# Sliding-window attention followed by a spectral mixing layer, on one core: a fixed engine order, full-size value and spectrum matmuls, paired transposes and one mask table

## The chip, the core and the metric

One core of a Trainium2 chip runs the whole program. The metric is device time in microseconds (us), the median of several runs. A run is "fast" or "slow" (slow: over 1.5% above the fastest of the same kernel); all runs quoted here are fast ones. The names of the engines in the profile are PE (TensorE, matmuls), PEld (its weight loads), DVE (VectorE), ACT (ScalarE), POOL (GpSimd) and SP (the DMA queue). SBUF is the on-chip memory in which the program keeps its tiles, PSUM the one that takes the results of matmuls.

## The reference, cut to what matters

```python
# q, k, v: (8 batches, 8 heads, 576 positions, 64); 64 modes; d_model 512
scores = q @ k.T / 8 + alibi_bias          # only 0 <= i - j < 128 is kept
attn   = softmax(scores);  x = (attn @ v), heads joined: (8, 576, 512)
X = rfft(x, axis=1)[:, :64]
Y = einsum('bmd,mde->bme', X, w_r + 1j*w_i)     # 64 modes, 128 MB of float32 weights
u = x + irfft(Y, n=576)
out = u + relu(u @ w_ch)
```

## The kernel before

The program has three stages. **Attention** goes through 16 units, each of one batch and four heads (a batch is two units), and fills `x` and then the spectrum `XC`. The **modes** stream 128 weight tiles of 1 MB through eight buffers. The **finish** makes the output tiles. In attention the engines' instructions are ordered by a scheduler; only the DMA queue's order is fixed (`manual_schedule(engines={SP})`).

```python
# the loop of attention; unit u is scored while unit u-1 takes its values
for u in range(n + 1):
    if u + 2 < n: at.load(u + 2)
    if u < n and (u % 2 == 1 or u == n - 2): load_w()
    if u < n:     at.scores(u, (0, 1))         # PE scores, ACT exp, DVE mask multiply
    if u + 1 < n: at.casts(u + 1)              # POOL: q, k, v to bf16
    if u > 0:     at.values(u - 1, 0)          # PE values, DVE normalise
    if u + 1 < n: at.transposes(u + 1, 0)      # PE transposes of q, ACT copy
    if u < n:     at.scores(u, (2, 3))
    if u > 0:     at.values(u - 1, 1)
    if u + 1 < n: at.transposes(u + 1, 1)      # PE transposes of k, DVE copy
    if u > 0 and u % at.NG == 0: at.spectrum(u // at.NG - 1)

def casts(self, u, eng=None):                  # cut
    (eng or nc.gpsimd).tensor_copy(qc, qr); (eng or nc.gpsimd).tensor_copy(kc, kr)
    vb = self.vb[u % 3]                        # three v buffers, freed by values()
    nc.gpsimd.tensor_copy(vb[:, :FULL, :, :D], vr[:, :FULL])
    nc.gpsimd.tensor_copy(vb[:TAIL, FULL, :, :D], vr[:TAIL, FULL])

# scores, per key tile kt:
nc.scalar.activation(att[:, kt], sc, AF.Exp, scale=1.0 / math.sqrt(D))
nc.vector.tensor_tensor(out=att[:, kt], in0=att[:, kt], in1=mask..., op=ALU.mult)

# values: after the full-width tiles of a head, the last 64 queries
nc.tensor.matmul(av[row, h, 260:325], lhsT=att[:, FULL-1, e, h*256+P : h*256+192], ...)
nc.tensor.matmul(av[row, h, 260:325], lhsT=att[:TAIL, FULL-1, e, h*256+192 : h*256+256], ...)
```

The softmax here doesn't subtract the row's maximum and nothing guards it: scores larger than these inputs give would overflow.

## Time and profile before

The median is 579.49 us (578.26 to 580.91, 4 runs). The stage borders are read from the timeline and from the instructions of the weight tiles.

| Stage, from the profiles | before | after |
|---|---|---|
| attention, until the first mode's matmul starts | 213.9 us | 199.0 us |
| modes, until the last weight tile's last matmul starts | 307.8 us | 310.2 us |
| finish, until the end | 55.5 us | 52.7 us |

Part 2 of the page of the kernel before cuts the span into 40 slices of 14.4 us. PEclk is the granted clock of PE in tenths (9 is 90% or more), DMA the busy tenths of the DMA engines. Part 4 says which work made up the chain that ended last.

```profile
PEclk9996655555555559786687889798877867676999
DMA  9998657759520019999999999999999999990666
...
DMA 42%; PE 32%; DVE 14%; ACT 6%; POOL 2%; issue 2%; SPq 0%; POOLq 0%; ACTq 0%
DMA w<-in_moe_w_i_dram 41%; PE acc L418 6%; DVE att L229 4%; PE av L249 4%; ACT att L227 3%; PE sc L222 3%; PE xt L289 3%; PE tp L197 2%; PE av L254 2%; PE av L258 2%; DVE x_full L268 2%; PE av L245 2%; PE zz L447 1%; PE mm L474 1%; DVE Zs L455 1%
```

From the sixteenth slice on DMA is full: the modes wait for weights, 41% of the span. The two zeros just before are a hole in which nothing is loaded, because all eight weight buffers are full and attention has not ended. So the modes' stream can't start earlier than attention's end, and what attention saves, the program saves.

The next view gives busy us of each engine in stretches of the kernel before (columns in its second line): two of attention, one of the modes.

```profile
core 0: us, PE busy (x) PEld busy (x) DVE busy (x) ACT busy (x) POOL busy (x), PEclk, DMA share, GB/s
100.00:120.00 20.00, 15.80 (x183) 11.02 (x179) 12.47 (x22) 10.27 (x11) 7.22 (x7) 0.50 0.77 229
120.00:140.00 20.00, 15.81 (x157) 10.32 (x156) 12.30 (x26) 8.34 (x10) 6.87 (x7) 0.50 0.65 198
230.00:250.00 20.00, 12.25 (x50) 5.26 (x49) 2.46 (x6) 1.73 (x4) 0.00 (x0) 0.74 1.01 423
```

No engine is full in attention, and PE's granted clock is 0.50. It is a loop of waits: scores, exp, mask, values, normalise, copies. A batch takes about 24 us (20.9 to 25.1 from the start of one batch's spectrum to that of the next, but for the last).

PE's timeline within the values of one head (start, length, what): the full-width matmuls follow each other every 50 to 60 ns, and each of the two 64-wide ones (L254, L258), and the first full-width one after them, comes 180 to 190 ns after its forerunner.

```profile
101.17 0.24 PE L245 MATMUL av<-vb_131,att 128*128 128x65 bf16 x1
101.23 0.25 PE L249 MATMUL av<-vb_131,att 128*128 128x65 bf16 x1
101.41 0.26 PE L254 MATMUL av<-vb_131,att 128*64 128x65 bf16 x1
101.60 0.26 PE L258 MATMUL av<-vb_131,att 64*64 64x65 bf16 x1
101.79 0.24 PE L249 MATMUL av<-vb_131,att 128*128 128x65 bf16 x1
```

The Trainium skill (TensorEngine Tiling (Array Packing), Key Properties) says that changing the tiling mode drains TensorE. The trace fits this, and adds a size: at half clock about 130 ns more than the usual spacing for each change. That all of it is the drain was not separated.

DVE's timeline at the start of the kernel before: a copy of 128x768 took 0.54 us once, and 5.88 us the next time, when POOL ran casts one after the other beside it. The first scores had to wait for the copy behind it. The last line is a mask multiply of the steady part, with no cast on POOL beside it: 0.69 us.

```profile
13.53 0.54 DVE L154 COPY maskB<-maskA 128x768 bf16<-128x768 bf16 x1
14.36 5.88 DVE L154 COPY maskB<-maskA 128x768 bf16<-128x768 bf16 x1 [0.29 <-POOL maskA L147]
20.17 1.34 DVE L201 COPY qkT_134<-tp 128x1152 bf16<-128x1152 bf16 x1
...
114.31 0.69 DVE L229 TENSOR_TENSOR att<-att,maskA 128x1024 bf16<-128x1024 bf16 x1
```

### The profile page before, as it was taken

The numbers are of one execution on the slowest core, as the hardware profiler recorded it, in microseconds if no ns is written. First come the engines' busy times: TensorE is split into PE (matmuls) and PEld (weight loads), VectorE is DVE, ScalarE is ACT, GpSimd is POOL, SyncE is SP. The second block draws the span as 40 slices with busy tenths as digits, with TensorE's granted clock in tenths as the row PEclk, the third lists the DMA queues.
The fourth block names the chain that finished last, engine by engine and source line by source line (L and its number), as shares of the span: only waits on it lengthen the run. The fifth ranks groups of instructions, "written<-read, shape, count | busy, mean of one in ns | idle before, by whom it ended". The sixth has DMA issues, their size and how long they took to land.

```text
span 577.3 us, 6872 instructions
## 1 busy us (share of the span) xinstructions
PE 398.7 (69%) x2677; PEld 208.6 (36%) x2694; DVE 208.7 (36%) x385; ACT 153.3 (27%) x214; POOL 91.7 (16%) x115
## 2 busy tenths in 40 slices
PE   1387679787788768477567646767664766666884
PEld 1255456555555534233233322323322322222331
DVE  5766666755656562101110111232011000003665
ACT  4344433453335403011001101221110100002554
POOL 5622242433231020000000000000000000000444
PEclk9996655555555559786687889798877867676999
DMA  9998657759520019999999999999999999990666
GB/s 255 297 274 263 197 150 237 243 132 246 154 108 1 1 68 398 423 419 422 423 419 422 420 421 421 421 421 357 423 422 421 422 420 423 421 396 20 212 209 217
DMA packets 71089, 173.48 MB, mean 301 GB/s; under 512 B 41360, under 2 KB 41360, under 8 KB 54672
## 3 DMA queue, kind: packets, MB, share of 16 engines
q1 hardware_dynamic: 71056, 173.03, 79.7%
q8 instruction: 21, 0.34, 0.2%
q14 instruction: 12, 0.10, 0.1%
HBM read 163.58 MB, written 9.44 MB: 300 GB/s over the span
## 4 chain that ended last, share of the span: by engine, by line
DMA 42%; PE 32%; DVE 14%; ACT 6%; POOL 2%; issue 2%; SPq 0%; POOLq 0%; ACTq 0%
DMA w<-in_moe_w_i_dram 41%; PE acc L418 6%; DVE att L229 4%; PE av L249 4%; ACT att L227 3%; PE sc L222 3%; PE xt L289 3%; PE tp L197 2%; PE av L254 2%; PE av L258 2%; DVE x_full L268 2%; PE av L245 2%; PE zz L447 1%; PE mm L474 1%; DVE Zs L455 1%
## 5 line engine op out<-in xcount | busy, mean ns | idle before, releaser
L418 PE MATMUL acc<-w,XC 128*32 128x512 bf16 x512 | 140.4, 452 | 56.9 <-DMA w<-in_moe_w_i_dram 32.9
L418 PEld LDWEIGHTS <-XC 128*32 128x32 bf16 x512 | 55.6, 141 | 122.6 <-issue 102.4
L227 ACT ACTIVATE att<-sc 128x1024 bf16<-128x1024 f32 x64 | 61.9, 1028 | 54.7 <-PE sc L222 54.7
L498 POOL TENSOR_TENSOR r<-r,x_full 128x512 f32<-128x512 f32 x16 | 18.5, 1157 | 338.1 <-ACT r L494 332.7
L427 DVE CAST yq<-acc 128x512 bf16<-128x512 f32 x16 | 11.1, 692 | 166.6 <-PE acc L418 166.6
L474 PE MATMUL mm<-wch,xT 128*128 128x512 bf16 x133 | 44.0, 455 | 9.2 <-DVE xT L471 8.9
L249 PEld LDWEIGHTS <-att 128*128 128x128 bf16 x256 | 25.6, 122 | 45.0 <-DVE x_tail L274 27.1
L229 DVE TENSOR_TENSOR att<-att,maskA 128x1024 bf16<-128x1024 bf16 x48 | 37.3, 777 | 12.1 <-ACT att L227 11.7
L476 ACT CAST XW<-mm 128x512 bf16<-128x512 f32 x36 | 21.1, 586 | 76.7 <-PE mm L474 76.7
L471 DVE COPY xT<-tr 128x512 bf16<-128x512 bf16 x36 | 15.3, 425 | 71.1 <-PE tr L469 71.1
L436 ACT COPY YT<-tr 128x128 bf16<-128x128 bf16 x8 | 5.8, 728 | 99.4 <-DVE YT L436 99.4
L469 PE MATMUL tr<-ident,x_full 128*128 128x128 bf16 x128 | 16.7, 272 | 18.9 <-ACT YT L439 12.6
L503 DVE TENSOR_TENSOR o<-yy,r 128x512 f32<-128x512 f32 x36 | 23.5, 687 | 14.8 <-POOL r L498 12.2
L222 PE MATMUL sc<-qkT_134 64*128 64x256 bf16 (+2 forms) x160 | 17.4, 361 | 15.8 <-DVE qkT_134 L201 13.0
L439 ACT COPY YT<-tr 128x64 bf16<-128x64 bf16 x16 | 5.8, 530 | 81.3 <-DVE YT L439 77.8
L474 PEld LDWEIGHTS <-xT 128*128 128x128 bf16 x144 | 12.8, 109 | 34.5 <-DVE xT L471 21.8
L494 ACT ACTIVATE r<-mm 128x512 f32<-128x512 f32 x36 | 21.1, 597 | 14.8 <-PE mm L483 11.3
L469 PEld LDWEIGHTS <-x_full 128*128 128x128 bf16 x128 | 13.2, 124 | 29.2 <-issue 19.5
L289 PE MATMUL xt<-F,x_full 128*128 128x128 bf16 x128 | 19.6, 308 | 5.5 <-DVE qkT_135 L201 4.2
L197 PE MATMUL tp<-ident,qc 128*64 128x128 bf16 x288 | 19.0, 314 | 5.5 <-DVE qc L183 5.5
L249 PE MATMUL av<-vb_131,att 128*128 128x65 bf16 x96 | 14.6, 242 | 11.5 <-DVE x_tail L274 10.3
L268 DVE TENSOR_TENSOR x_full<-av,rec 128x512 bf16<-128x512 f32 x32 | 22.0, 689 | 0.6
(109 smaller groups left out, 557.2 us busy)
## 6 DMA issues: line engine op xcount, KB each, us to landing
w<-in_moe_w_r_dram SPq DMA_DIRECT2D x64, 1024.0 KB, 15.4
w<-in_moe_w_i_dram SPq DMA_DIRECT2D x64, 1024.0 KB, 16.6
qr<-in_q_dram SPq DMA_DIRECT2D x16, 576.0 KB, 4.9
kr<-in_k_dram SPq DMA_DIRECT2D x16, 576.0 KB, 5.6
vr<-in_v_dram SPq DMA_DIRECT2D x64, 128.0 KB, 3.4
out_dram<-o SPq DMA_DIRECT2D x32, 256.0 KB, 2.1
vr<-in_v_dram SPq DMA_DIRECT2D x16, 64.0 KB, 3.9
w<-in_moe_w_ch_dram SPq DMA_DIRECT2D x1, 1024.0 KB, 6.2
```

Source lines behind the costliest of these rows:

```text
L197: nc.tensor.transpose(tp[64 * e : 64 * e + 64, j], src[:, e, j * D : (j + 1) * D], self.ident)
L222: nc.tensor.matmul(sc[:, e, h * 256 + c0 : h * 256 + c0 + n], lhsT=qkT[row, 1, h, k0 : k0 + P], rhs=qkT[row, 0, h, q0 : q0 + n],)
L227: nc.scalar.activation(att[:, kt], sc, AF.Exp, scale=1.0 / math.sqrt(D))
L229: nc.vector.tensor_tensor(out=att[:, kt], in0=att[:, kt], in1=mask.rearrange("p (e h) n -> p e (h n)", e=2), op=ALU.mult,)
L249: nc.tensor.matmul(dst, lhsT=att[:, qt, e, h * 256 : h * 256 + P], rhs=vb[:, qt, hv, : D + 1], start=(qt == 0), stop=True,)
L268: nc.vector.tensor_tensor(out=self.x_full[:, b, :, cs].rearrange("p t (h d) -> p h t d", h=2), in0=tiles[:, :, :, :D], in1=rec.unsqueeze(- ...
L289: nc.tensor.matmul(xt[:, a].rearrange("p r m -> p (r m)"), lhsT=self.x_full[:, b, st, a::4], rhs=self.F[:, st], start=(st == 0), stop=False,)
L418: nc.tensor.matmul(acc[32 * j : 32 * j + 32], lhsT=XC[:, c0 : c0 + 31 * NM + 1 : NM], rhs=w[:, a].bitcast(BF16)[:, 1::2], start=(ri == 0 a ...
L469: nc.tensor.transpose(tr[:, dt], x[:, dt * P : (dt + 1) * P], ident)
L474: nc.tensor.matmul(mm, lhsT=xT[:, dt], rhs=wch[:, dt], start=(dt == 0), stop=(dt == 3))
L476: nc.scalar.copy(XW[:, i], mm)
L503: nc.vector.tensor_tensor(out=o, in0=yy, in1=r, op=ALU.add)
```

## The change

The intent is to shorten the loop of attention: no tile mode changes in the values and spectra, fewer and larger DVE instructions, the k copy shared by two engines, and an order of all engines that is the program's own. `x_full` and `x_tail` become one array `x`, whose tail rows are padded with zero rows of the table; the odd batches' tails are then joined by a POOL copy. Cut to its core (renamings, reshapes, the sine helper and the start's reorder left out):

```diff
 # transposes: e and d side by side, one 128-wide transpose in place of two
-            for e in range(2):
-                nc.tensor.transpose(tp[64 * e : 64 * e + 64, j], src[:, e, j * D : (j + 1) * D], self.ident)
+            nc.tensor.transpose(tp[:, j], src[:, j].rearrange("p e d -> p (e d)"), self.ident)
 # the k copy
-        eng = nc.scalar.copy if w == 0 else nc.vector.tensor_copy
+            nc.scalar.copy(dst[:, 0], src[:, 0])
+            nc.vector.tensor_copy(dst[:, 1], src[:, 1])
 # values: the tail is a fifth full-width tile; one reciprocal and one multiply
-            for qt in range(FULL):
+            for qt in range(FULL + 1):
+                    terms = [(a(FULL - 1, P - 64 * odd), FULL - 1), (a(FULL - 1, 192 - 64 * odd), FULL)]
-        nc.vector.reciprocal(rect[row], av[row, :, 324])          # and its multiply
 # spectrum: five full-width matmuls; then the tails are joined
+        if b % 2:
+            nc.gpsimd.tensor_copy(self.x[:64, b, FULL], self.x[:64, b - 1, FULL])
 # one mask table; the last key tile's mask in two pieces
-            mask = (self.maskA if kt < FULL - 1 else self.maskB)[:, 4 * g : 4 * g + 4]
+        for c0, m0, n in ((0, 0, 256),) if kt < FULL - 1 else ((0, 0, 192), (192, 0, 64)):
 # the forward table's padding
+    nc.vector.memset(F[:64, FULL + 1], 0.0)
+    nc.vector.tensor_copy(F[64:, FULL + 1], F[64:, FULL])
+    nc.vector.memset(F[64:, FULL], 0.0)
 # order
+        actx.enter_context(tc.manual_schedule(engines=ALL))
+            if u + 1 < n: at.casts(u + 1)      # now first in the unit
+            if u == 12: nc.gpsimd.tensor_copy(wch, wq[0])
 # finish
+        spectra(1, 0)
         for bp in range(B // 2):
-            spectra(1, bp)
+            if bp + 1 < B // 2: spectra(1, bp + 1)
```

More of the change, by code (lines that the diff above doesn't have):

```diff
@@ L16 @@
 SP = mybir.EngineType.SP
+ALL = {mybir.EngineType.PE, mybir.EngineType.Activation, mybir.EngineType.DVE,
+       mybir.EngineType.Pool}
 P = 128
@@ L35, in _sin_of @@
     y = pool.tile(list(ang.shape), FP32, tag="sin_y")
-    nc.vector.tensor_scalar_mul(y, ang, 1.0 / S)
-    nc.vector.tensor_scalar(y, y, MAGIC, -MAGIC, op0=ALU.add, op1=ALU.add)
-    nc.vector.scalar_tensor_tensor(
-        out=y, in0=y, scalar=-float(S), op0=ALU.mult, in1=ang, op1=ALU.add
-    )
+    nc.vector.tensor_scalar(y, ang, 1.0 / S, MAGIC, op0=ALU.mult, op1=ALU.add)
+    nc.vector.tensor_scalar(y, y, -MAGIC, -float(S), op0=ALU.add, op1=ALU.mult)
+    nc.vector.tensor_tensor(out=y, in0=y, in1=ang, op=ALU.add)
     nc.scalar.activation(dst, y, AF.Sin, scale=TWO_PI / S)
@@ L69, in _forward_table @@
         nc.vector.tensor_scalar_add(ang[:, :, ri, :], prod, float(S) / (4 - 2 * ri))
-    _sin_of(nc, pool, F.rearrange("p a b -> p (a b)"),
+    _sin_of(nc, pool, F[:, : FULL + 1].rearrange("p a b -> p (a b)"),
             ang.rearrange("p a b c -> p (a b c)"), S)
+    nc.vector.memset(F[:64, FULL + 1], 0.0)
+    nc.vector.tensor_copy(F[64:, FULL + 1], F[64:, FULL])
+    nc.vector.memset(F[64:, FULL], 0.0)
 def _inverse_table(nc, pool, FT, S, NM):
@@ L109, with __init__ @@
 class _Attention:
-    def __init__(self, tc, ctx, q, k, v, consts, x_full, x_tail, XC):
+    def __init__(self, tc, ctx, q, k, v, consts, x, XC):
         self.tc, self.nc = tc, tc.nc
@@ L115, in __init__ @@
         self.ident, self.F, self.ek = consts
-        self.x_full, self.x_tail, self.XC = x_full, x_tail, XC
+        self.x, self.XC = x, XC
         B, H, S, _ = q.shape
@@ L123, in __init__ @@
         fix = ctx.enter_context(tc.tile_pool(name="afix", bufs=1))
-        self.maskA = fix.tile([P, H, 2 * P], BF16, name="maskA")
-        self.maskB = fix.tile([P, H, 2 * P], BF16, name="maskB")
+        self.mask = fix.tile([P, H, 2 * P], BF16, name="mask")
         self.vb = [fix.tile([P, FULL + 1, 4, D + 2], BF16, name=f"vb{i}") for i in range(3)]
         self.qkT = [fix.tile([P, 2, 2, (FULL + 1) * P], BF16, name=f"qkT{i}") for i in range(2)]
-        self.loaded, self.cast, self.atts = {}, {}, {}
+        self.att = [fix.tile([P, FULL * 8 * P + 64], BF16, name=f"att{i}") for i in range(2)]
+        self.loaded, self.cast = {}, {}
     def fixtures(self):
+        nc = self.nc
         for t in self.vb:
-            self.nc.gpsimd.memset(t[:, :, :, D : D + 1], 1.0)
+            nc.gpsimd.memset(t[:, :, :, D : D + 1], 1.0)
+            nc.gpsimd.memset(t[TAIL:, FULL, :, :D], 0.0)
         for t in self.qkT:
-            self.nc.gpsimd.memset(t[:, 1, :, self.S :], 0.0)
+            nc.gpsimd.memset(t[:, 1, :, self.S :], 0.0)
+        for t in self.att:
+            nc.gpsimd.memset(t[:, FULL * 8 * P :], 1.0)
     def masks(self, h0):
@@ L140, in masks @@
             hs = slice(h0, h0 + 2)
-            nc.gpsimd.affine_select(
-                out=self.maskA[:, hs, :P],
-                in_=self.ek[:, 0, hs].unsqueeze(-1).broadcast_to([P, 2, P]),
-                compare_op=ALU.is_ge, fill=0.0, base=0,
-                pattern=[[0, 2], [1, P]], channel_multiplier=-1,
-            )
-            nc.gpsimd.affine_select(
-                out=self.maskA[:, hs, P:],
-                in_=self.ek[:, 1, hs].unsqueeze(-1).broadcast_to([P, 2, P]),
-                compare_op=ALU.is_ge, fill=0.0, base=-1,
-                pattern=[[0, 2], [-1, P]], channel_multiplier=1,
-            )
-        hs = slice(h0 - 2, h0 + 2)
-        nc.vector.tensor_copy(self.maskB[:, hs, :192], self.maskA[:, hs, :192])
-        nc.vector.tensor_copy(self.maskB[:, hs, 192:], self.maskA[:, hs, :64])
+            for n, (sign, base) in enumerate(((1, 0), (-1, -1))):
+                nc.gpsimd.affine_select(
+                    out=self.mask[:, hs, n * P : n * P + P],
+                    in_=self.ek[:, hs, n : n + 1].broadcast_to([P, 2, P]),
+                    compare_op=ALU.is_ge, fill=0.0, base=base,
+                    pattern=[[0, 2], [sign, P]], channel_multiplier=-sign,
+                )
     def load(self, u):
@@ L160, in load @@
         hs = slice(4 * g, 4 * g + 4)
-        qr = self.raw.tile([P, 2, TPP * D], FP32, tag="qr")
-        kr = self.raw.tile([P, 2, TPP * D], FP32, tag="kr")
+        qr = self.raw.tile([P, 2, TPP, D], FP32, tag="qr")
+        kr = self.raw.tile([P, 2, TPP, D], FP32, tag="kr")
         vr = self.raw.tile([P, FULL + 1, 4, D], FP32, tag="vr")
@@ L165, in load @@
             nc.sync.dma_start(
-                out=dst,
+                out=dst.rearrange("p e j d -> p e (j d)"),
                 in_=src[b, hs].rearrange("(e h) (p j) d -> (h p) e (j d)", h=2, j=TPP),
@@ L180, in casts @@
         qr, kr, vr = self.loaded.pop(u)
-        qc = self.mid.tile([P, 2, TPP * D], BF16, tag="qc")
-        kc = self.mid.tile([P, 2, TPP * D], BF16, tag="kc")
-        (eng or nc.gpsimd).tensor_copy(qc, qr)
-        (eng or nc.gpsimd).tensor_copy(kc, kr)
+        qc = self.mid.tile([P, TPP, 2, D], BF16, tag="qc")
+        kc = self.mid.tile([P, TPP, 2, D], BF16, tag="kc")
+        for dst, src in ((qc, qr), (kc, kr)):
+            (eng or nc.gpsimd).tensor_copy(dst.rearrange("p j e d -> p e j d"), src)
         vb = self.vb[u % 3]
@@ L192, in transposes, with scores @@
         src = self.cast[u][w]
-        qkT = self.qkT[u % 2]
         tp = self.ps.tile([P, TPP, P], BF16, tag="tp")
         for j in range(TPP):
-            for e in range(2):
-                nc.tensor.transpose(
-                    tp[64 * e : 64 * e + 64, j], src[:, e, j * D : (j + 1) * D], self.ident
-                )
-        eng = nc.scalar.copy if w == 0 else nc.vector.tensor_copy
-        eng(
-            qkT[:, w, :, : self.S].rearrange("q h (p j) -> q h p j", j=TPP),
-            tp.rearrange("q j (h p) -> q h p j", h=2),
-        )
-    def scores(self, u, kts):
+            nc.tensor.transpose(tp[:, j], src[:, j].rearrange("p e d -> p (e d)"), self.ident)
+        dst = self.qkT[u % 2][:, w, :, : self.S].rearrange("q h (p j) -> q h p j", j=TPP)
+        src = tp.rearrange("q j (h p) -> q h p j", h=2)
+        if w == 0:
+            nc.scalar.copy(dst, src)
+        else:
+            nc.scalar.copy(dst[:, 0], src[:, 0])
+            nc.vector.tensor_copy(dst[:, 1], src[:, 1])
+    def scores(self, u, kt):
         nc = self.nc
@@ L209, in scores @@
         qkT = self.qkT[u % 2]
-        if u not in self.atts:
-            self.atts[u] = self.mid.tile([P, FULL, 2, 2 * 2 * P], BF16, tag="att", name="att")
-        att = self.atts[u]
-        for kt in kts:
-            sc = self.ps.tile([P, 2, 512], FP32, tag="sc", bufs=2)
-            for h in range(2):
-                spans = [(kt * P, kt * P, 0, min(2 * P, self.S - kt * P))]
-                if kt == FULL - 1:
-                    spans.append((FULL * P, FULL * P, 192, TAIL))
-                for k0, q0, c0, n in spans:
-                    for e in range(2):
-                        row = slice(64 * e, 64 * e + 64)
-                        nc.tensor.matmul(
-                            sc[:, e, h * 256 + c0 : h * 256 + c0 + n],
-                            lhsT=qkT[row, 1, h, k0 : k0 + P],
-                            rhs=qkT[row, 0, h, q0 : q0 + n],
-                        )
-            nc.scalar.activation(att[:, kt], sc, AF.Exp, scale=1.0 / math.sqrt(D))
-            mask = (self.maskA if kt < FULL - 1 else self.maskB)[:, 4 * g : 4 * g + 4]
+        att = self.att[u % 2][:, kt * 8 * P : (kt + 1) * 8 * P]
@@ new lines, in scores @@
+        sc = self.ps.tile([P, 2, 512], FP32, tag="sc", bufs=2)
+        for h in range(2):
+            spans = [(kt * P, kt * P, 0, min(2 * P, self.S - kt * P))]
+            if kt == FULL - 1:
+                spans.append((FULL * P, FULL * P, 192, TAIL))
+            for k0, q0, c0, n in spans:
+                for e in range(2):
+                    row = slice(64 * e, 64 * e + 64)
+                    nc.tensor.matmul(
+                        sc[:, e, h * 256 + c0 : h * 256 + c0 + n],
+                        lhsT=qkT[row, 1, h, k0 : k0 + P],
+                        rhs=qkT[row, 0, h, q0 : q0 + n],
+                    )
@@ L229, in scores @@
+        nc.scalar.activation(
+            att, sc.rearrange("p e n -> p (e n)"), AF.Exp, scale=1.0 / math.sqrt(D)
+        )
+        heads = att.rearrange("p (h n) -> p h n", h=4)
+        mask = self.mask[:, 4 * g : 4 * g + 4]
+        for c0, m0, n in ((0, 0, 256),) if kt < FULL - 1 else ((0, 0, 192), (192, 0, 64)):
             nc.vector.tensor_tensor(
-                out=att[:, kt], in0=att[:, kt],
-                in1=mask.rearrange("p (e h) n -> p e (h n)", e=2), op=ALU.mult,
+                out=heads[:, :, c0 : c0 + n], in0=heads[:, :, c0 : c0 + n],
+                in1=mask[:, :, m0 : m0 + n], op=ALU.mult,
@@ L236, in values @@
         b, g = self.units[u]
-        row = slice(64 * (b % 2), 64 * (b % 2) + 64)
-        att, vb = self.atts[u], self.vb[u % 3]
+        odd = b % 2
+        att, vb = self.att[u % 2], self.vb[u % 3]
         av = self.ps.tile([P, 2, 512], FP32, tag="av")
@@ L241, in values, with a @@
             hv = 2 * e + h
-            for qt in range(FULL):
+            def a(kt, c0):
+                o = ((kt * 2 + e) * 2 + h) * 256 + c0
+                return att[:, o : o + P]
+            for qt in range(FULL + 1):
                 dst = av[:, h, qt * 65 : qt * 65 + 65]
-                if qt:
+                if qt == 0:
+                    terms = [(a(0, 0), 0)]
+                elif qt < FULL:
+                    terms = [(a(qt - 1, P), qt - 1), (a(qt, 0), qt)]
+                else:
+                    terms = [(a(FULL - 1, P - 64 * odd), FULL - 1),
+                             (a(FULL - 1, 192 - 64 * odd), FULL)]
+                for n, (lhsT, kt) in enumerate(terms):
@@ L245, in values @@
                     nc.tensor.matmul(
-                        dst, lhsT=att[:, qt - 1, e, h * 256 + P : h * 256 + 2 * P],
-                        rhs=vb[:, qt - 1, hv, : D + 1], start=True, stop=False,
-                    )
-                nc.tensor.matmul(
-                    dst, lhsT=att[:, qt, e, h * 256 : h * 256 + P],
-                    rhs=vb[:, qt, hv, : D + 1], start=(qt == 0), stop=True,
-                )
-            dst = av[row, h, 260:325]
-            nc.tensor.matmul(
-                dst, lhsT=att[:, FULL - 1, e, h * 256 + P : h * 256 + 192],
-                rhs=vb[:, FULL - 1, hv, : D + 1], start=True, stop=False,
-            )
@@ L258, in values @@
-            nc.tensor.matmul(
-                dst, lhsT=att[:TAIL, FULL - 1, e, h * 256 + 192 : h * 256 + 256],
-                rhs=vb[:TAIL, FULL, hv, : D + 1], start=False, stop=True,
-            )
+                        dst, lhsT=lhsT, rhs=vb[:, kt, hv, : D + 1],
+                        start=(n == 0), stop=(n == len(terms) - 1),
+                    )
         cs = slice((4 * g + 2 * e) * D, (4 * g + 2 * e + 2) * D)
-        rec = self.mid.tile([P, 2, FULL], FP32, tag="rec")
-        rect = self.mid.tile([P, 2], FP32, tag="rect")
@@ L265, in values @@
-        tiles = av[:, :, :260].rearrange("p h (t n) -> p h t n", n=65)
+        rec = self.mid.tile([P, 2, FULL + 1], FP32, tag="rec")
+        tiles = av[:, :, :325].rearrange("p h (t n) -> p h t n", n=65)
         nc.vector.reciprocal(rec, tiles[:, :, :, D])
-        nc.vector.reciprocal(rect[row], av[row, :, 324])
         nc.vector.tensor_tensor(
-            out=self.x_full[:, b, :, cs].rearrange("p t (h d) -> p h t d", h=2),
+            out=self.x[:, b, :, cs].rearrange("p t (h d) -> p h t d", h=2),
@@ L270, in values @@
             in0=tiles[:, :, :, :D],
-            in1=rec.unsqueeze(-1).broadcast_to([P, 2, FULL, D]),
-            op=ALU.mult,
-        )
-        nc.vector.tensor_tensor(
-            out=self.x_tail[row, b // 2, cs].rearrange("p (h d) -> p h d", h=2),
-            in0=av[row, :, 260:324],
-            in1=rect[row].unsqueeze(-1).broadcast_to([64, 2, D]),
+            in1=rec.unsqueeze(-1).broadcast_to([P, 2, FULL + 1, D]),
             op=ALU.mult,
@@ L284, in spectrum @@
         NM = self.F.shape[2] // 2
-        row = slice(64 * (b % 2), 64 * (b % 2) + 64)
         xt = self.ps.tile([P, 4, 2, NM], FP32, tag="tp")
         for a in range(4):
-            for st in range(FULL):
+            for st in range(FULL + 1):
                 nc.tensor.matmul(
                     xt[:, a].rearrange("p r m -> p (r m)"),
-                    lhsT=self.x_full[:, b, st, a::4], rhs=self.F[:, st],
-                    start=(st == 0), stop=False,
-                )
-            nc.tensor.matmul(
-                xt[:, a].rearrange("p r m -> p (r m)"),
-                lhsT=self.x_tail[row, b // 2, a::4], rhs=self.F[row, FULL],
-                start=False, stop=True,
-            )
+                    lhsT=self.x[:, b, st, a::4],
+                    rhs=self.F[:, st + (b % 2 if st == FULL else 0)],
+                    start=(st == 0), stop=(st == FULL),
+                )
         view = self.XC[:, : 4 * NC * NM].rearrange("p (a c m) -> p a c m", a=4, c=NC)
@@ L323 @@
     const = ctx.enter_context(tc.tile_pool(name="const", bufs=1))
-    x_full = const.tile([P, B, FULL, DM], BF16, name="x_full")
-    x_tail = const.tile([P, B // 2, DM], BF16, name="x_tail")
+    x = const.tile([P, B, FULL + 1, DM], BF16, name="x")
     XC = const.tile([P, 4 * NC * NM + 16 * NM], BF16, name="XC")
     ident = const.tile([P, P], BF16, name="ident")
-    F = const.tile([P, FULL + 1, 2 * NM], BF16, name="F")
-    ek = const.tile([P, 2, H], FP32, name="ek")
-    with tc.tile_pool(name="setup", bufs=1) as pool:
+    F = const.tile([P, FULL + 2, 2 * NM], BF16, name="F")
+    ek = const.tile([P, H, 2], FP32, name="ek")
+    wch = const.tile([P, 4, DM], BF16, name="wch")
+    with tc.tile_pool(name="setup", bufs=1) as pool, tc.manual_schedule(engines=ALL):
         make_identity(nc, ident)
-        _forward_table(nc, pool, F, S)
-        kv_i = pool.tile([P, 1], I32)
-        nc.gpsimd.iota(kv_i, [[0, 1]], base=0, channel_multiplier=1)
-        kv = pool.tile([P, 1], FP32)
+        kv_i = pool.tile([P, 2], I32)
+        nc.gpsimd.iota(kv_i, [[-P, 2]], base=0, channel_multiplier=1)
+        kv = pool.tile([P, 2], FP32)
         nc.vector.tensor_copy(kv, kv_i)
@@ L339 @@
             slope = 2.0 ** (-8.0 * (h + 1) / H)
-            nc.scalar.activation(ek[:, 0, h : h + 1], kv, AF.Exp, scale=slope)
-            nc.vector.tensor_scalar_mul(
-                ek[:, 1, h : h + 1], ek[:, 0, h : h + 1], math.exp(-P * slope)
-            )
+            nc.scalar.activation(ek[:, h], kv, AF.Exp, scale=slope)
+        _forward_table(nc, pool, F, S)
     wpool = ctx.enter_context(tc.tile_pool(name="w", bufs=NW))
@@ L360 @@
     with ExitStack() as actx:
-        at = _Attention(tc, actx, q, k, v, (ident, F, ek), x_full, x_tail, XC)
+        at = _Attention(tc, actx, q, k, v, (ident, F, ek), x, XC)
+        actx.enter_context(tc.manual_schedule(engines=ALL))
         n = len(at.units)
@@ L376 @@
                 load_w()
-            if u < n:
-                at.scores(u, (0, 1))
             if u + 1 < n:
                 at.casts(u + 1)
+            for kt in (0, 1):
+                if u < n:
+                    at.scores(u, kt)
             if u > 0:
@@ L384 @@
                 at.transposes(u + 1, 0)
-            if u < n:
-                at.scores(u, (2, 3))
+            for kt in (2, 3):
+                if u < n:
+                    at.scores(u, kt)
             if u > 0:
@@ L392 @@
                 at.spectrum(u // at.NG - 1)
+            if u == 12:
+                nc.gpsimd.tensor_copy(wch, wq[0])
     with ExitStack() as mctx:
@@ L396 @@
         FT = fix.tile([P, 2, S], BF16, name="FT")
-        wch = fix.tile([P, 4, DM], BF16, name="wch")
         YT = fix.tile([P, 2, 4, B, 2, HM], BF16, name="YT")
@@ L405 @@
         XW = big.tile([P, 9 * (B // 2), DM], BF16, name="XW")
-        nc.gpsimd.tensor_copy(wch, wq[0])
         load_w()
@@ L460 @@
                 for bb in range(2):
-                    tiles.append((x_full[:, 2 * bp + bb, st], [2 * bp + bb], st))
-            tiles.append((x_tail[:, bp], [2 * bp, 2 * bp + 1], FULL))
+                    tiles.append((x[:, 2 * bp + bb, st], [2 * bp + bb], st))
+            tiles.append((x[:, 2 * bp + 1, FULL], [2 * bp, 2 * bp + 1], FULL))
         def project(i):
@@ L518 @@
                 todo = i + 1
+        spectra(1, 0)
         for bp in range(B // 2):
-            spectra(1, bp)
+            if bp + 1 < B // 2:
+                spectra(1, bp + 1)
             for i in range(9 * bp, 9 * bp + 9):
```

## The prediction

> **What bounds it now** (windows and chain of waits). Three stages:
> (1) Attention, until the last spectrum's copy ends near 213.8 us.
> (2) The modes, until the last weight tile lands at 520.6 us. DMA is full (421 GB/s), PE waits for weights; the chain has 41% of the span there. From about 180 to 212 us nothing is loaded: all weight buffers are full.
> (3) The finish, 57 us of PE/ACT/DVE latency.
> About 120 weight tiles of 1.05 MB must stream after the first mode frees its buffers (landing 306.8 us after that mode starts, in either kernel), so stage 2 is a constant and a microsecond saved in attention is saved overall.
>
> **Attention** takes about 24.2 us per batch (two units). Its granted clock is 0.50 almost throughout: 65-column matmuls follow each other every 54 ns. The Trainium skill (TensorE: Matmul & The Clock Gate, Part 1) says that half rate is the default and sustained activity lifts it; this trace shows only blips (28 ns spacing near 44-46 us). No engine is full: PE 78% (drains included), DVE 62%, ACT 43%. A serial loop bounds it: scores, exp, mask, values, normalise, transposes, copies, next scores.
>
> **What the change does, by the trace's durations.**
> - Full-width tails: where a 64-wide tail stands in the stream, spacing goes from 54 to about 190 ns, about 0.4 us per head, 1.6 us of PE per unit.
> - Spectrum: 3.1 us to about 2.15 (20 x 107 ns): 1 us per batch, on the chain.
> - Paired transposes: the halves already overlap (18 in 1.12 us); about 0.15 us each.
> - The k copy (DVE, 1.36 us, PE waiting 0.9-1.4 us behind it) splits into halves of about 0.7 on ACT and DVE: 0.65 us per unit, on the chain.
> - Normalisation: four DVE instructions (1.36 us) become two (about 1.0), twice a unit.
> - Mask table: the 5.88 us maskB copy, stuck behind POOL's casts, held the first scores until 21.6 us; they should start near 13.5. The last key tile pays one extra DVE instruction, about 0.1 us.
> - Added: padding memsets, and a POOL copy per odd batch waiting for a spectrum, under 1 us on average.
>
> Added up in the fixed order: 19.5-20 us per batch instead of 24.2, about -33 us, and -8 us at the start. Attention should end near 173 us (160-185): about -41 us, nearly all critical. DMA busy time in attention is about 126 us, so loads should not bind, though early units come close.
> - The earlier wch cast preloads one more tile, but the old kernel fetched it at 212.6 us before the first mode freed anything: gain near 0.
> - Spectra one pair ahead remove short waits at three pair changes, but delay the first tiles: -1 to -3 us.
>
> **Prediction: 536 us**, 8 in 10 between 521 and 552. Faster by over 2%: 0.96; same 0.03; slower 0.01.
>
> **Right if:** unbroken 54 ns spacing in values; first scores at 12-16 us; batch period 19-21 us; weight stream restarts near 173 us; DMA-bound stage still about 305 us; finish 53-57 us.
>
> **Wrong if:**
> - DVE masks meet POOL's casts more often. The skill (GPSIMD Engine Reference, Specifications) says POOL shares SBUF interfaces with DVE instructions of two SBUF inputs; the trace agrees: masks of 0.69 us took up to 2.9 us beside casts. That could cost 1-2 us per unit: 545-560.
> - The denser PE stream lifts the clock for long stretches: 17 us per batch, 515-520.
> - The fixed order makes an engine wait where the scheduler had found a gap.
> - The modes' order on PE changes so that DMA idles.

## The result

The changed kernel takes 563.07 us (559.54 to 564.97, 4 runs), against 579.49 us. The ratio is 0.971, with a 95% interval of 0.966 to 0.976. Ratios here and below are the mean time of one kernel's fast runs over that of the kernel before in the same rounds, so they are not quite the ratio of the medians quoted. It is faster, but by 16.4 us where 43.5 us were predicted, and the time lies above the predicted range of 521 to 552 us.

The modes take 310.2 us, 2.4 us more, the finish 52.7 us, 2.8 us less. Attention ends at 199.0 us, 14.9 us earlier, where 41 us were predicted.

The page of the changed kernel, the same four lines:

```profile
PEclk9976766776766678688679867898976866685999
DMA  9998469669550059999999999998999999990476
...
DMA 44%; PE 23%; DVE 19%; ACT 9%; issue 2%; POOL 1%; SPq 0%; POOLq 0%; ACTq 0%; DVEq 0%
DMA w<-in_moe_w_i_dram 43%; PE acc L409 6%; DVE att_134 L229 6%; PE sc L218 3%; DVE att_133 L229 3%; PE av L259 3%; ACT att_133 L223 3%; DVE x L267 3%; ACT att_134 L223 2%; PE xt L281 2%; PE tp L196 2%; PE zz L438 2%; PE mm L465 1%; DVE Zs L446 1%; ACT r L485 1%
```

PE's share of the chain fell from 32 to 23%, as intended, and DVE's rose from 14 to 19%. The mask multiplies (L229, two buffers' names) went from 4% of the span to 9%. The stretches of the changed kernel:

```profile
100.00:120.00 20.00, 12.95 (x178) 9.99 (x175) 13.68 (x21) 12.53 (x15) 5.67 (x7) 0.74 0.40 113
120.00:140.00 20.00, 8.17 (x106) 6.50 (x107) 15.83 (x20) 8.12 (x10) 10.33 (x11) 0.65 1.02 305
```

The second is unlike the first: PE does half as much as before the change, while DVE and POOL are busiest. The values themselves are as predicted: on PE's timeline of the changed kernel all 18 matmuls of a values step stand in one piece, with no change of mode.

```profile
129.00 1.17 PE L259 MATMUL av<-vb_128,att_134 128*128 128x65 bf16 x18
129.98 1.15 PE L196 MATMUL tp<-ident,qc 128*128 128x128 bf16 x9
```

The lost time is in DVE's masks. It is not spread evenly: measured from spectrum to spectrum, three batches take 19.3 to 19.7 us, as predicted, and the three between them 23.8 to 25.9 us. Each of these slow three starts behind the new POOL copy of an odd batch's tail (L292), and its first mask takes 5.3, 5.3 and 7.1 us. This is the longest case in the changed kernel, first POOL's timeline, then DVE's (start, length):

```profile
160.27 0.61 POOL L292 COPY x<-x 64x512 bf16<-64x512 bf16 x1 [11.64 <-PE xt L281]
160.83 1.89 POOL L385 CAST wch<-w 128x2048 bf16<-128x2048 f32 x1
162.66 1.14 POOL L185 CAST qc<-qr 128x1152 bf16<-128x1152 f32 x1
163.76 1.14 POOL L185 CAST kc<-kr 128x1152 bf16<-128x1152 f32 x1
...
167.27 1.14 POOL L185 CAST kc<-kr 128x1152 bf16<-128x1152 f32 x1
```

```profile
161.84 7.71 DVE L229 TENSOR_TENSOR att_134<-att_134,mask 128x1024 bf16<-128x1024 bf16 x2 [0.56 <-ACT att_134 L223]
169.48 0.21 DVE L266 RECIPROCAL rec<-av 128x10 f32<-128x10 f32 x1
```

Two masks of 0.7 us together take 7.71 us, the first of them alone 7.11; they end 1.1 us after POOL's last cast does. All 80 mask instructions of the changed kernel stand for 76.4 us on DVE's timeline, and nine groups of them take more than 2.2 us. The same thing happens to a small copy at the start, the new padding of the table:

```profile
12.37 6.07 DVE L74 COPY F<-F 64x128 bf16<-64x128 bf16 x1 [0.73 <-ACT F L41]
18.51 0.11 DVE L75 MEMSET F<- 64x64 uint32 x1
18.66 0.76 DVE L203 COPY qkT_131<-tp 128x576 bf16<-128x576 bf16 x1
```

The first two score matmuls of the changed kernel ran at 12.9 us, as predicted (12 to 16 us), and then PE waited until 19.5 us for the half copy behind this one.

### The profile page after: what moved, and what is told of

Same layout as the page of the kernel before. It is cut to its first block, busy times and chain, and to the rows that moved or that the text cites. A ratio compares the mean times of both kernels' runs of the same rounds, so it can differ in the third digit from the quotient of the medians.

```text
span 562.0 us, 6337 instructions
## 1 busy us (share of the span) xinstructions
PE 359.8 (64%) x2406; PEld 186.4 (33%) x2406; DVE 212.2 (38%) x328; ACT 162.6 (29%) x230; POOL 94.8 (17%) x124
## 4 chain that ended last, share of the span: by engine, by line
DMA 44%; PE 23%; DVE 19%; ACT 9%; issue 2%; POOL 1%; SPq 0%; POOLq 0%; ACTq 0%; DVEq 0%
DMA w<-in_moe_w_i_dram 43%; PE acc L409 6%; DVE att_134 L229 6%; PE sc L218 3%; DVE att_133 L229 3%; PE av L259 3%; ACT att_133 L223 3%; DVE x L267 3%; ACT att_134 L223 2%; PE xt L281 2%; PE tp L196 2%; PE zz L438 2%; PE mm L465 1%; DVE Zs L446 1%; ACT r L485 1%
## 5 line engine op out<-in xcount | busy, mean ns | idle before, releaser
L409 PE MATMUL acc<-w,XC 128*32 128x512 bf16 x512 | 144.7, 459 | 53.9 <-DMA w<-in_moe_w_i_dram 30.1
L489 POOL TENSOR_TENSOR r<-r,x 128x512 f32<-128x512 f32 x18 | 20.8, 1155 | 338.4 <-ACT r L485 337.6
L418 DVE CAST yq<-acc 128x512 bf16<-128x512 f32 x16 | 11.1, 692 | 168.1 <-PE acc L409 168.1
L465 PE MATMUL mm<-wch,xT 128*128 128x512 bf16 x144 | 48.8, 474 | 5.3 <-DVE xT L462 5.2
L229 DVE TENSOR_TENSOR att_134<-att_134,mask 128x1024 bf16<-128x1024 bf16 (+2 forms) x40 | 42.7, 1099 | 9.4 <-ACT att_134 L223 9.4
L229 DVE TENSOR_TENSOR att_133<-att_133,mask 128x1024 bf16<-128x1024 bf16 (+2 forms) x40 | 33.8, 867 | 22.5 <-ACT att_133 L223 22.5
L223 ACT ACTIVATE att_133<-sc 128x1024 bf16<-128x1024 f32 x32 | 31.1, 1027 | 23.3 <-PE sc L218 23.3
L281 PE MATMUL xt<-F,x 128*128 128x128 bf16 x160 | 15.4, 277 | 29.5 <-DVE qkT_132 L203 28.4
L223 ACT ACTIVATE att_134<-sc 128x1024 bf16<-128x1024 f32 x32 | 31.1, 1028 | 2.5 <-PE sc L218 2.4
L460 PE MATMUL tr<-ident,x 128*128 128x128 bf16 x144 | 18.4, 268 | 18.8 <-ACT YT L430 12.5
L494 DVE TENSOR_TENSOR o<-yy,r 128x512 f32<-128x512 f32 x36 | 23.6, 687 | 13.5 <-POOL r L489 6.8
L267 DVE TENSOR_TENSOR x<-av,rec 128x640 bf16<-128x640 f32 x32 | 26.4, 825 | 1.1
L460 PEld LDWEIGHTS <-x 128*128 128x128 bf16 x144 | 14.6, 123 | 30.5 <-issue 19.2
L281 PEld LDWEIGHTS <-x 128*128 128x128 bf16 x160 | 14.3, 134 | 30.2 <-DVE x L267 26.4
```

The source lines that it names most:

```text
L223: nc.scalar.activation(att, sc.rearrange("p e n -> p (e n)"), AF.Exp, scale=1.0 / math.sqrt(D))
L229: nc.vector.tensor_tensor(out=heads[:, :, c0 : c0 + n], in0=heads[:, :, c0 : c0 + n], in1=mask[:, :, m0 : m0 + n], op=ALU.mult,)
L267: nc.vector.tensor_tensor(out=self.x[:, b, :, cs].rearrange("p t (h d) -> p h t d", h=2), in0=tiles[:, :, :, :D], in1=rec.unsqueeze(-1).br ...
L281: nc.tensor.matmul(xt[:, a].rearrange("p r m -> p (r m)"), lhsT=self.x[:, b, st, a::4], rhs=self.F[:, st + (b % 2 if st == FULL else 0)], ...
L409: nc.tensor.matmul(acc[32 * j : 32 * j + 32], lhsT=XC[:, c0 : c0 + 31 * NM + 1 : NM], rhs=w[:, a].bitcast(BF16)[:, 1::2], start=(ri == 0 a ...
L460: nc.tensor.transpose(tr[:, dt], x[:, dt * P : (dt + 1) * P], ident)
```

## The experiments

Theory A: DVE instructions with two SBUF inputs (the masks), and its copies from SBUF to SBUF, wait while POOL runs casts. The Trainium skill (SBUF — State Buffer, "SBUF: two separate sides") says that a DVE instruction in a two-port mode, or one with two SBUF inputs beside a GpSimd one that reads SBUF, shares a pair of ports with GpSimd under an exclusive lock: whichever starts first has it, and the other one blocks. The traces above fit this (7.11 us for a mask, 6.07 us for a copy). In its first form the theory blamed the new POOL copy (L292): it waits up to 12.6 us for a spectrum, and the casts queue up behind it. Theory B: the fixed order makes engines wait where the scheduler had found a gap. Theory C: the new shapes (split masks, strided casts) are slow by themselves.

"Mask time" below is the sum of the 80 mask instructions' lines on DVE's timeline. "Attention" is the start of the first mode's matmul in the profile.

| Run | us, median | ratio to before | attention | mask time |
|---|---|---|---|---|
| changed kernel | 563.1 | 0.971 | 199.0 | 76.4 |
| x1_copy_late | 574.7 | 0.990 | 207.7 | 81.9 |
| x2_table_act | 557.1 | 0.960 | 193.2 | 75.6 |
| x3_no_qkcast | 534.1 | 0.923 | 170.2 | 54.6 |
| x4_sched | 557.8 | 0.961 | 194.7 | 72.8 |
| y8_gate3 | 534.0 | 0.921 | 168.1 | 49.0 |
| y9_gate1 | 553.5 | 0.957 | 190.3 | 66.6 |
| y10_gate3_act | 529.0 | 0.915 | 163.7 | 51.1 |
| y11_nocast_act | 533.9 | 0.922 | 171.1 | 54.4 |

### The late tail copy (x1_copy_late)

```diff
-        if b % 2:
-            nc.gpsimd.tensor_copy(self.x[:64, b, FULL], self.x[:64, b - 1, FULL])
+        for b in range(1, B, 2):               # behind the last unit
+            nc.gpsimd.tensor_copy(x[:64, b, FULL], x[:64, b - 1, FULL])
```

> The GpSimd copy of the 64 tail rows of x, which in the changed kernel stands in GpSimd's queue behind every second spectrum, is moved behind the last unit; nothing else changes. Theory A (DVE's mask multiplies are kept off the SBUF interface for as long as GpSimd runs casts back to back, and the copy's wait for the spectrum bunches six casts into one run): the three masks of 5.2 to 7.1 us go, only ordinary collisions of 1 to 4 us stay; attention ends 9 to 14 us earlier than 199 us, total 549 to 554 us. Theory B (the fixed engine order makes DVE and PE wait, GpSimd does not matter): no change, 560 to 565 us. Theory C (the split and strided mask and cast forms are slow by themselves): no change.

It was a miss: 574.7 us, 11.6 us slower. The long stalls went, as expected, but now eleven of the 16 units have one of 3.7 to 5.5 us (here with 1.4 us of masks in it). POOL's and DVE's timelines in one unit of this run:

```profile
101.79 1.04 POOL L187 CAST vb<-vr 128x1024 bf16<-128x1024 f32 x1 [9.66 <-PE av L259]
102.78 0.85 POOL L188 CAST vb<-vr 64x256 bf16<-64x256 f32 x1
103.58 1.14 POOL L185 CAST qc<-qr 128x1152 bf16<-128x1152 f32 x1
104.68 1.14 POOL L185 CAST kc<-kr 128x1152 bf16<-128x1152 f32 x1
```

```profile
101.95 4.48 DVE L229 TENSOR_TENSOR att<-att,mask 128x1024 bf16<-128x1024 bf16 x3 [0.96 <-ACT att L223]
```

The bracket on the first POOL line is the clue. POOL had been idle 9.66 us, until the values matmuls freed a v buffer; then v, q and k are cast in one run. The values of that step end just before masks 2 and 3 of the unit become due. So taking away the bunching behind the tail copy did not take away the loss. In the changed kernel about half of what the masks lose against their length beside a quiet POOL, 16 of some 32 us, falls on the first masks behind that copy; in this run nearly all of it, 33 of 37 us, falls on the two masks of the units' last key tile. The batches show the exchange: all of the first five now take 24.3 to 26.3 us, the short ones of 19.3 to 19.7 are gone. The bunching had apparently kept casts away from the masks of every other batch. The first form of theory A had the interference right and its cause at best half right.

### The table copy on ScalarE (x2_table_act)

```diff
-    nc.vector.tensor_copy(F[64:, FULL + 1], F[64:, FULL])
+    nc.scalar.copy(F[64:, FULL + 1], F[64:, FULL])
```

> The small copy inside the forward table (64x128, 6.07 us on DVE at 12.4 us, beside GpSimd's memset and casts) goes to ScalarE. Theory A: the first full set of scores starts near 14 us in place of 19.5 us, total 4 to 6 us less, 557 to 559 us. Theories B and C: no change beyond 1 us.

It took 557.1 us, 6.0 us less, and attention ended 5.8 us earlier. The first full set of scores began at 13.7 us. The wait partly came back: unit 0's five masks then took 7.20 us beside the same casts.

### No q and k casts (x3_no_qkcast)

```diff
-        for dst, src in ((qc, qr), (kc, kr)):
-            (eng or nc.gpsimd).tensor_copy(dst.rearrange("p j e d -> p e j d"), src)
+            for e in range(2):
+                nc.tensor.transpose(tp[64 * e : 64 * e + 64, j], src[:, e, j].bitcast(BF16)[:, 1::2], self.ident)
```

> The q and k casts are taken off GpSimd: the transposes read the upper half of the float32 words (truncated, so the result is slightly less exact), two halves per transpose as in the kernel before. GpSimd keeps the v casts and the tail copy, about 1.5 us a unit in place of 3.7. Theory A: excess of the mask multiplies over their own 0.7 us falls from about 30 us to under 10 us; total 539 to 547 us. Theory B: no gain, and up to 5 us lost by the split transposes, 562 to 568 us. Theory C: masks stay long; no gain.

It took 534.1 us and was still correct: 29.0 us less than the changed kernel, 5 us better than expected. Mask time fell by 21.8 us. A batch takes 18.8 to 20.4 us, 19.7 on average, close to the 19.5 to 20 us that the prediction had added up. This fits theory A. Theory B is refuted as the main cause, and so are the split masks of theory C: the engine order and the masks' shapes are those of the changed kernel. The strided casts of theory C went out with the edit, so this run does not clear them; y8_gate3 below, which keeps them, does.

### The scheduler's order again (x4_sched)

```diff
-        actx.enter_context(tc.manual_schedule(engines=ALL))
```

> Only the fixed order of attention is undone: the scheduler orders all engines but the DMA queue's there, everything else is as changed. Theory B (the order is what costs): at least 10 us faster, 553 us or less. Theory A (GpSimd's runs cost, in any order): long masks of 3 to 7 us are still there, total within 5 us of 563 us.

It took 557.8 us, 5.3 us less, just outside the band that theory A allowed, and far from the 10 us of theory B. Groups of masks of 6.5, 8.0, 8.0 and 7.7 us are still there. The fixed order therefore costs at most about 5 us of the missing 27.

### Two gates, first try (x8_gate3, x9_gate1, x10_gate3_act, x11_gate3_act_late)

If the moment counts and not the amount, it must be enough to move the casts. A copy of one column from the masked scores holds POOL until a chosen mask is done.

```diff
+    def gate(self, u, kt):
+        end = (kt + 1) * 8 * P
+        self.nc.gpsimd.tensor_copy(self.mark, self.att[u % 2][:, end - 1 : end])
 # in the loop; casts(1) stands ahead of it, and casts(u + 1) is taken out
             for kt in (2, 3):
                 if u < n: at.scores(u, kt)
+            if u + 2 < n:
+                at.gate(u, 3)          # gate(u, 1) after the first two masks in x9
+                at.casts(u + 2)
```

> All GpSimd work stays (q, k and v casts, tail copies); only its moment changes. A one-column GpSimd copy that reads the last masked column of a unit stands before the casts for the unit after next, so each run of casts (3.7 us) starts when DVE has finished the unit's fourth mask and works on PSUM (normalise, k copy). Theory A in its new form (what costs is that each run of casts is released by the values matmuls just before masks 2 and 3, which DVE then can't do; the amount of GpSimd work and its bunching do not matter): the sum of the masks falls from 76 us to 48 to 55 us, a batch takes 19 to 20.5 us, total 536 to 544 us. Theory A in its old form (amount of GpSimd work): masks stay near 76 us, total 558 to 568 us. Theory B (order): no change.

> The same one-column copy and the same casts, but placed after the unit's second mask, so that every run of casts starts just before masks 2 and 3. New form of theory A: each unit has a stall of about 3 us in masks 2 and 3, mask sum 80 to 95 us, total 565 to 580 us, as the run with the late tail copies. If the gate itself (a longer lead of the casts, or the extra instruction) made the other gated kernel fast, this one is as fast.

> Gate after the fourth mask, and the forward table's small copy on ScalarE. The two gains add: 5 to 6 us less than with the gate alone, 530 to 538 us, at or below the kernel without q/k casts.

> As the last, with the GpSimd tail copies behind the last unit. With the casts gated, the copy no longer stands before casts that a unit needs: within 2 us of the kernel before it (531 to 538 us). If the wait for the spectrum were harmful by itself, 5 us or more are gained.

All four gave wrong results, and 603 to 614 us. This was my mistake: the casts of unit u+2 write the v buffer (u+2) % 3, which is that of unit u-1, before that unit's last values are issued. The values then read the wrong data and had to wait for the casts. Nothing follows from these four.

### Two gates, with a fourth v buffer (y8_gate3, y9_gate1)

```diff
-        self.vb = [... for i in range(3)]      # and vb[u % 3]
+        self.vb = [... for i in range(4)]      # and vb[u % 4]
```

> The gate after the fourth mask again, now with four v buffers in place of three: in the first try the casts for unit u+2 were written, in program order, before the values of unit u-1 had read the same buffer, which was a mistake of the edit (wrong result, and values that waited for casts). Expected as written there. Phase form of theory A (each run of casts is released just before masks 2 and 3): mask sum 48 to 55 us in place of 76, a batch 19 to 20.5 us, total 536 to 544 us. Amount form: masks near 76 us, 558 to 568 us. Theory B (order): no change.

> Same gate copy, same four v buffers, but the gate reads the second mask's output, so each run of casts starts just before masks 2 and 3. Phase form: a stall of about 3 us a unit, mask sum 80 to 95 us, total 565 to 580 us. If the fourth v buffer or the longer lead of the casts made the other gated kernel fast, this one is as fast.

With the gate behind the fourth mask the kernel takes 534.0 us, below the expected band, with mask time 49.0 us, and is correct. A batch takes 18.3 us on average. POOL does all the work of the changed kernel plus the gate copies. POOL's and DVE's timelines in one unit:

```profile
105.52 0.19 POOL L237 COPY mark<-att 128x1 bf16<-128x1 bf16 x1 [5.62 <-DVE rec L271]
105.64 1.14 POOL L186 CAST qc<-qr 128x1152 bf16<-128x1152 f32 x1
...
108.81 0.85 POOL L189 CAST vb<-vr 64x256 bf16<-64x256 f32 x1
```

```profile
104.60 0.76 DVE L230 TENSOR_TENSOR att<-att,mask 128x768 bf16<-128x768 bf16 x2 [0.23 <-ACT att L224]
105.28 0.21 DVE L271 RECIPROCAL rec<-av 128x10 f32<-128x10 f32 x1
105.53 0.82 DVE L272 TENSOR_TENSOR x<-av,rec 128x640 bf16<-128x640 f32 x1
106.27 0.75 DVE L204 COPY qkT<-tp 128x576 bf16<-128x576 bf16 x1
108.46 1.75 DVE L230 TENSOR_TENSOR att<-att,mask 128x1024 bf16<-128x1024 bf16 x2 [1.44 <-ACT att L224]
```

(The view names the reciprocal as what released the gate copy; the copy reads the mask's output, and DVE's mask ended at 105.36 us.) The run of casts now falls into the stretch in which DVE reads PSUM (normalise, k copy) and then waits for the next exp. The normalise of 0.82 us and the copy of 0.75 us are as long beside casts as without them.

With the gate after the second mask, the same instructions and buffers give 553.5 us and 66.6 us of mask time. The direction is as expected, the size is not: I had expected 3 us a unit and 565 to 580 us. DVE's timeline shows why:

```profile
105.15 2.79 DVE L230 TENSOR_TENSOR att<-att,mask 128x1024 bf16<-128x1024 bf16 x3 [0.96 <-ACT att L224]
107.86 0.21 DVE L271 RECIPROCAL rec<-av 128x10 f32<-128x10 f32 x1
```

The casts there started at 103.45 us, 1.7 us ahead of the masks, so only the rest of the run was in their way, 1.4 us a unit. The pair settles the cause: the same POOL work, moved within the unit by one condition, is worth 19.5 us. The other 9.6 us between the changed kernel and y9_gate1 come with the fourth buffer, the longer lead of the casts and the end of the bunching (its batches are even, 20.4 to 21.5 us); no run separates these.

### The gate and the ScalarE copy (y10_gate3_act), and neither q/k casts nor the DVE copy (y11_nocast_act)

> Gate after the fourth mask, four v buffers, and the forward table's small copy on ScalarE: the gains add, 5 to 6 us less than with the gate alone, 530 to 538 us.

529.0 us (526.1 to 532.2): the gains nearly add. This is the fastest sound version but for the equal one below (z4); it beats the kernel before by 8.5% and the changed one by 34 us.

> No q and k casts (truncated halves read by the transposes), and the small copy on ScalarE. 4 to 6 us less than without the latter: 528 to 530 us. The batch period stays 19.5 to 20 us, the sum that was predicted for the change without contention.

533.9 us, no gain over x3_no_qkcast: a miss, which theory A explains afterwards. In x3_no_qkcast's trace, without the q and k casts at the start, the DVE copy takes 0.97 us and not 6.07, so there was little left to gain.

### One term at a time, from the 529 us kernel (z1 to z4)

Was the prediction right but for the casts, or did errors cancel? Each run undoes one part of the change in y10_gate3_act.

```diff
 # z1: spectra(1, bp) stands again right before the tiles of pair bp
 # z2: nc.vector.tensor_copy(dst, src) for the whole of k
 # z3: values' tails 64 wide, two reciprocals and two multiplies (spectra stay full width)
 # z4: two 64-wide transposes for each 128-wide one
```

> From the gated kernel with the ScalarE table copy (529 us): only the finish's order is undone, each pair's spectra again stand right before that pair's tiles. Prediction's term: 1 to 3 us lost, 530 to 532 us, with the time from the last weight matmul to the end near 55 us in place of 52. If the order is worth nothing: within 1 us.

> From the same kernel: the k copy is whole again on DVE (1.36 us) and not in halves. Prediction's term: 0.65 us a unit on the chain, 16 units, 8 to 11 us lost, 537 to 540 us. If the copy is hidden, under 3 us.

> From the same kernel: the values' tails are 64 wide again (two matmuls a head in tile modes of their own) with four normalising instructions, as in the kernel before; the spectra stay full width. Prediction's terms: 1.6 us of PE and 0.7 us of DVE a unit; if all of it is on the chain 30 to 37 us lost (559 to 566 us); if only the half of it that stands before the next wait, 15 to 20 us (544 to 549 us).

> From the same kernel: each transpose again in two halves. Prediction's term: 0.15 us for each of 32 sets, at most 5 us lost, 529 to 534 us.

| Undone | us, median | ratio to before | lost against 529.0 | predicted for the term |
|---|---|---|---|---|
| z1 spectra ahead | 532.7 | 0.921 | 3.7 | 1 to 3 |
| z2 halved k copy | 543.8 | 0.940 | 14.8 | 8 to 11 |
| z3 full-width values, merged normalisation | 549.8 | 0.951 | 20.7 | 30 to 37 if all on the chain, 15 to 20 if half |
| z4 paired transposes | 528.7 | 0.914 | -0.3 | up to 5 |

The runs of one kernel differ by 2 to 6 us here, so z1 and z4 are sizes only within that. In z1's profile the time from the last weight tile's matmul to the end is 55.0 us in place of 53.4; the rest of its loss lies in attention, which the edit does not touch. The k copy is worth more than its own 0.6 us a unit: in z2's profile a batch takes 20.5 us in place of 18.3, which is 1.1 us a unit. A likely reason is that ACT's half comes early enough for the first head's scores to start, but no run separates this. The full-width spectrum was undone in no run.

## Why the prediction was wrong

**What bounds it: right.** Attention's saving passed to the whole: 14.9 us in attention, 16.4 us in all. In the 529 us kernel attention ends at 163.7 us and the modes still take 307.3 us.

**The terms of PE: about right, in part by luck.** Values run unbroken. With contention removed, a batch takes 18.8 to 20.4 us (x3) or 18.3 us (y8), where 19.5 to 20 us were added up. But the sum took half clock, and the clock rose (see below), so the agreement does not prove each term. Single terms were off both ways: the k copy was undersized (14.8 us for 8 to 11), the paired transposes gave nothing, the values lie between the two readings.

**The step that failed** is the sum as it was put: "Added up in the fixed order: 19.5-20 us per batch instead of 24.2, about -33 us, and -8 us at the start." It took the overlap of DVE's masks with POOL's casts as free: no term of it lets a mask take longer than when POOL is quiet, and the new POOL copy was put at "under 1 us on average", while the batches behind it took 4 to 6 us more than the others. In the changed kernel the masks took 76.4 us in place of the 49.0 us of the gated kernel, 27.4 us more. That this is so near the miss (563.1 less 536) is partly chance: the table copy at the start cost another 5 to 6 us, and freed of both the kernel takes 529.0 us, 7 us less than predicted. So the overlap cost some 34 us, and the rest of the sum was 7 us too high. The prediction named this risk ("DVE masks meet POOL's casts more often ... 545-560") but left it out of the middle and of most of the range. And "they should start near 13.5" met the same cause: the first two scores ran at 12.9 us, the rest at 19.5 us, behind a table copy of 6.07 us. The kernel before had shown the same with its 5.88 us copy. I had credited the change with removing that copy, and overlooked that it adds another one in the same place.

**Why the moment got worse** is argued, not shown. In the kernel before, the masks of attention's steady part (62 of them, 26 to 205 us) took 52.2 us in the groups view: 0.84 us each on average, with a median of 0.69. So some contention was there already, and could have been priced. There 8 of the 15 k casts waited for PE's transposes, so that POOL's runs were often cut in two, as here:

```profile
104.94 1.59 POOL L183 CAST qc<-qr 128x1152 bf16<-128x1152 f32 x1 [0.48 <-POOL vb_131 L187]
110.51 1.14 POOL L184 CAST kc<-kr 128x1152 bf16<-128x1152 f32 x1 [3.98 <-PE tp L197]
```

In the changed kernel none of the 15 waited, and each run of casts is in one piece. The fixed order alone does not explain it: under the scheduler's order (x4_sched) the masks still took 72.8 us.

**The finish** was rightly put: 2.8 us less, predicted 1 to 3. **The extra weight tile** gave nothing, as predicted. The modes' 2.4 us more were not predicted. At 380 to 390 us in the changed kernel the DMA rate falls to 261 GB/s, where PE catches up after the first half's spectra; the kernel before has a smaller dip of the same kind (329 GB/s at 395 to 405 us). No run looked into it.

**The clock** is a side effect that the prediction gave as a chance only: it was 0.50 through most of attention before, and 0.57 to 0.84 after, in stretches of 20 us from 40 us on. What it is worth was not separated.

## What to carry to other kernels

Where DVE and GpSimd work side by side on SBUF, a saving on PE can be lost to when GpSimd's work is released, and not only to how much of it there is: look on the timeline for DVE instructions several times their usual length, and see whether they end just behind a run of GpSimd instructions. Then give that run a moment in which DVE reads PSUM or waits; a one-column copy that reads the right tile is enough of a gate. Here the gate and its fourth buffer gained 29 us, of which the right moment was worth 19.5. When a change is costed from a trace, take the durations that an instruction has beside its new neighbours, not its best ones.

## What the Trainium skill lacked or had wrong

- SBUF — State Buffer, "SBUF: two separate sides": it says the lock is held for the whole instruction. Here a mask waited not for one GpSimd instruction but for a run of them: a mask of 0.7 us took 7.11 us, through seven casts. In other cases a mask got in before the run ended (three masks in 2.79 us, with the casts' run going on to 107.8 us). Which it will be, the page does not say, and these runs leave it open.
- VectorE: DVE Perf Modes has no warning that a small SBUF copy can wait as long as a large one: 64x128 bf16 took 6.07 us beside casts (128x768 took 5.88 us) and 0.97 us with fewer of them.
- TensorEngine Tiling (Array Packing), Key Properties: a change of tiling mode drains the engine; no size is given. Here matmuls came 180 to 190 ns apart at a change, and 50 to 60 ns apart without, at half clock.
- TensorE: Matmul & The Clock Gate, Part 1, has the clock lifted after some 3.4 us of sustained activity. In the kernel before, PE ran from 121.4 to 128.2 us, when transposes follow, without a listed wait after the first matmul, and the granted clock of that stretch is 0.50. So being busy, as the profile counts it, was not enough here; what is enough, no run here shows.
